# Cross attention and routed experts on one core: x of five batches transposed by the DMA crossbar, and a rebuilt opening

## The chip, the cores and the metric

The kernel runs on 1 core of a Trainium2 chip. Five engines work side by side, each with its own queue of instructions in order: TensorE (PE, with its weight loads PEld), VectorE (DVE), ScalarE (ACT), GpSimd (POOL) and SyncE (SP, which only issues DMAs). The core has 16 DMA engines. DMAs are issued from SP's queue, from ACT's, or from GpSimd's (software-generated, which can cast). The metric is the device time of the program in microseconds (us), as the median of the runs.

## The reference

Two stages. The first is an attention between x and a small state in both directions, for 8 batches and 8 heads, with S = 512, 32 state rows and D = 64:

```
scores  = scale * x @ state^T        ;  xread = softmax(scores)  @ state      (512 rows per batch)
scores2 = scale * state @ x^T        ;  sread = softmax(scores2) @ x          (32 rows per batch)
x2 = [xread, sread] as rows: 8 * 544 = 4352 rows of 512
```

The second is a mixture of 8 experts over these rows, in which every expert computes every row, and the weights P are balanced by 8 rounds of row and column normalisation (Sinkhorn):

```
P = exp(x2 @ w_gate - max), 8 rounds:  P /= row sums;  P /= column sums;  P *= N / E
out = sum over e of  P[:, e] * (relu(x2 @ w1[e]) @ w2[e])        w1: 512 x 1024, w2: 1024 x 512
```

The output has 4352 x 512 values in float32.

## The kernel before

**Heads.** Four of a batch's eight heads are worked at once, so there are 16 objects `Heads(k)`, two per batch: k = 2b + q. "Head k" below means such a group of four. Its steps are:

- `transpose` (L168): eight TensorE transposes of 128x128 (`xT_ps`), and one VectorE copy to `xT`
- `scores` (L178): two matmuls `sc_ps` of state (`stT`, 64 columns each) with `xT`; ScalarE takes exp with row sums to `E2`
- `rows` (L189): reciprocal `rrec` and normalised `En` on VectorE
- `columns` (L196): matmul `den_ps` with a matrix of ones, then Ln and Exp on ScalarE to `rcp`
- `flip` (L203): four transposes of `En` to `ET_ps`, copied to `ET` by VectorE
- `weights` (L210): `AT` = E2 times rcp on VectorE
- `read_x` (L213): eight matmuls `su_ps` of `x_nat` with `ET`, copied to `xs`

`beat(k)` (L482) strings head k's steps together with the transposes and scores of head k+1.

**Expert 0 beside attention.** xread is never formed: the product of state and W1 (`G`, from matmuls `g_ps`) is computed first, and layer 1 then multiplies `AT` with `G` (`hps`, then relu on ScalarE to `hT`). `state_times_w1(bp, w1h)` (L285) computes `G` for a pair of batches, in eight steps of one 128x512 product, whose two halves of 64 partitions go to the two batches in one copy each. For the first pair the copies of five steps are on ScalarE and of three on VectorE, for later pairs all are on VectorE. `layer1` (L335) has eight steps per batch, `layer2` (L357) has for each of four row tiles two steps of four matmuls (`yps`), and a copy to `acc`.

**Order.** All engine queues are written out by hand (`manual_schedule`): program order is queue order. After the hand-written start (the "opening", heads 0 and 1), `prologue` is the list of attention steps, cut into parts of two heads, and `units[c]` is the list of expert steps (layer 1 of batch c, layer 2 of batch c-1, and the `G` of a later pair). `weave` mixes a unit with its part of the prologue. I call such a mixture a unit below. Later experts (1 to 7) follow with a layer 2 of fewer products (`layer2_winograd`); the change doesn't touch them.

**Loads.** State and x come on SP's queue (`load_state` L83, `load_x` L92), in tiles `x_st` with three buffers, of which the two state tiles (`st_nat`) are two turns. `cast_x` (L100) makes fp16 `x_nat` (three buffers), on VectorE for batches 0 and 1 and on GpSimd after that. Weights come with a cast on GpSimd's queue (`load_w1`, `load_w2`). The start is gated so that they come one after another: a one-element copy on GpSimd holds W1 until the state is there, x of batch 1 until W1's first half is there, and W2 until W1's second half is there. `ahead(b)` (L553) stands at the first head of batch b-1, loads and casts x of batch b, and at b = 5 also starts the weights of expert 1. `prepare_state(g)` (L145) casts and transposes the state of four batches. `warm(n)` (L497) issues matmuls without a purpose but activity.

**The end of the attention stage** is near 122 us of the profile; after it SP carries the `G<-raw` copies of the later experts.

Of the kernel before, what the change touches and what calls it, by code (L numbers as in the profile page):

```python
# [10 lines left out]
FP32 = mybir.dt.float32  # L11
FP16 = mybir.dt.float16
# [6 lines left out]
def kernel(  # L19
# [9 lines left out]
    nc = tc.nc  # L29

    B, H, S, D = x.shape
    Ns = state.shape[2]
    Dm, E = moe_w_gate.shape
    F = moe_w1.shape[2]
    SB = S + Ns
    N = B * SB
    NKC = Dm // 128
    NFB = F // 128
    NTB = N // 128
    NSC = S // 128  # L40
    NQ = H // 4
    SR = B * S

    inv_sqrt_d = 1.0 / float(D) ** 0.5
# [3 lines left out]
    psM = ctx.enter_context(tc.tile_pool(name="psM", bufs=4, space=bass.MemoryType.PSUM))  # L48
# [6 lines left out]
    gp = ctx.enter_context(tc.tile_pool(name="gp", bufs=4))  # L55
# [7 lines left out]
    AT = persist.tile([128, NQ, SR], FP16, name="AT")  # L63
# [11 lines left out]
    actx = ExitStack()  # L75
    axs = actx.enter_context(tc.tile_pool(name="attn_xs", bufs=3))
    axp = actx.enter_context(tc.tile_pool(name="attn_x", bufs=3))
    asb = actx.enter_context(tc.tile_pool(name="attn_sb", bufs=2))
    ast = actx.enter_context(tc.tile_pool(name="attn_st", bufs=1))
    stT = ast.tile([128, B // 2, NKC, 2, 64], FP16, name="stT")  # L80
    st_nat = [axs.tile([128, H, D], FP32, name=f"st_nat{g}", tag="x_st") for g in range(2)]

    def load_state(g):  # L83
        for k in range(4):
            nc.sync.dma_start(out=st_nat[g][ds(32 * k, 32)],
                              in_=state[4 * g + k].rearrange("h n d -> n h d"))


    x_st = {}
    x_nats = {}  # L90

    def load_x(b, after=None):  # L92
        xv = x[b].rearrange("h (p s) d -> p h s d", s=NSC)
        for q in range(NQ):
            t = x_st[b, q] = axs.tile([128, 4, NSC, D], FP32, name="x_st", tag="x_st")
            if after is not None and q == 0:
                nc.gpsimd.tensor_copy(out=t[:1, 0, 0, :1], in_=after)
            nc.sync.dma_start(out=t, in_=xv[:, ds(4 * q, 4)])

    def cast_x(b, q):  # L100
        if q == 0:
            x_nats[b] = axp.tile([128, NKC, NSC, 2, D], FP16, name="x_nat", tag="x_nat")
        for par in range(2):
            (nc.vector if b < 2 else nc.gpsimd).tensor_copy(
                out=x_nats[b][:, 2 * q + par].rearrange("p s i d -> p i s d"),
                in_=x_st[b, q][:, ds(2 * par, 2)])

    def load_w1(e, after=None):
        w1h = mw.tile([128, NKC, F], FP16, name="w1h", tag="w1h")
# [51 lines left out]
    class Heads:  # L161
# [4 lines left out]
            self.odd = self.b % 2  # L166

        def transpose(self):  # L168
            xn = x_nats[self.b]
            xT_ps = psA.tile([128, 2, S], FP16, name="xT_ps", tag="a")  # L170
            for par in range(2):
                for sc in range(NSC):
                    nc.tensor.transpose(xT_ps[:, par, ds(128 * sc, 128)],  # L173
                                        xn[:, 2 * self.q + par, sc, :, :], identh)
            self.xT = asb.tile([128, 2, S], FP16, name="xT", tag="xT")
            nc.vector.tensor_copy(out=self.xT, in_=xT_ps)  # L176

        def scores(self):  # L178
# [34 lines left out]
        def read_x(self):  # L213
            xn = x_nats[self.b]
            su_ps = psA.tile([128, 2, 64], FP32, name="su_ps", tag="a")
            for par in range(2):
                for sc in range(NSC):
                    nc.tensor.matmul(su_ps[:, par, :], xn[:, 2 * self.q + par, sc, :, :],  # L218
                                     self.ET[:, sc, ds(64 * (par ^ self.odd), 64)],
                                     start=(sc == 0), stop=(sc == NSC - 1))  # L220
            for i in range(2):
                nc.vector.tensor_copy(
                    out=xs[ds(64 * i, 64), ds(2 * self.q, 2), ds(self.b * Ns, Ns)],
                    in_=su_ps[ds(64 * i, 64), :, ds(32 * i, 32)])
# [28 lines left out]
    def state_times_w1_four(g, w1h, split=False):  # L253
# [5 lines left out]
        def step(kc, fhs):  # L259
# [15 lines left out]
            if 1 in fhs:  # L275
                for b in range(4):
# [5 lines left out]
        return G, [partial(step, kc, fhs) for kc in range(NKC)  # L282
                   for fhs in ([(0,), (1,)] if split else [(0, 1)])]

    def state_times_w1(bp, w1h):  # L285

        G = []

        def step(kc, fh):
            if not G:  # L290
                G.extend(gp.tile([128, NQ, F], FP16, name="G", tag="G") for _ in range(2))
            g_ps = psM.tile([128, 512], FP32, name="g_ps", tag="m")
            nc.tensor.matmul(g_ps, stT[:, bp, kc, :, :], w1h[:, kc, ds(512 * fh, 512)])  # L293
            on_dve = bp > 0 or (kc, fh) in ((0, 0), (2, 0), (1, 1))
            evac = nc.vector.tensor_copy if on_dve else nc.scalar.copy
            for half in range(2):
                evac(out=G[half ^ (kc % 2)][ds(64 * half, 64), kc // 2, ds(512 * fh, 512)],  # L297
                     in_=g_ps[ds(64 * half, 64), :])

        return G, [partial(step, kc, fh) for fh in range(F // 512) for kc in range(NKC)]  # L300

# [33 lines left out]
    def layer1(c, w1h, G):  # L335

        tn = S if c < B else B * Ns
        h = []

        def step(fb):  # L340
            if not h:
                h.append((mh if c < B else mhs).tile([128, NFB, tn], FP16, name="hT", tag="hT"))
            hps = psM.tile([128, 512], FP32, name="hps", tag="m")
            if c < B:
                for q in range(NQ):
                    nc.tensor.matmul(hps[:, :tn], G[c % len(G)][:, q, ds(fb * 128, 128)],  # L346
                                     AT[:, q, ds(c * S, S)],
                                     start=(q == 0), stop=(q == NQ - 1))
            else:
                for kc in range(NKC):  # L350
                    nc.tensor.matmul(hps[:, :tn], w1h[:, kc, ds(fb * 128, 128)], xs[:, kc, :],  # L351
                                     start=(kc == 0), stop=(kc == NKC - 1))
            nc.scalar.activation(out=h[0][:, fb, :], in_=hps[:, :tn], func=AF.Relu)  # L353

        return h, [partial(step, fb) for fb in range(NFB)]
# [104 lines left out]
    def weave(a, b):  # L460

        steps, k = [], 0
        for i, f in enumerate(a):
            steps.append(f)
            while k < len(b) and k * len(a) < (i + 1) * len(b):
                steps.append(b[k])
                k += 1
        return steps + b[k:]

    def run(steps):  # L470
        for f in steps:
            f()
# [7 lines left out]
    heads = [Heads(k) for k in range(B * NQ)]  # L480
# [9 lines left out]

    warm_sb = ast.tile([128, S], FP16, name="warm_sb")
    nc.vector.memset(warm_sb, 0.0)
    warm_ps = psM.tile([128, S], FP32, name="warm_ps", tag="m")

    def warm(n):  # L497
        for _ in range(n):
            nc.tensor.matmul(warm_ps, warm_sb[:, :128], warm_sb)  # L499
# [3 lines left out]
    warm(11)  # L503
    identh = consts.tile([128, 128], FP16, name="identh")
    make_identity(nc, identh)
    headones = consts.tile([128, 128], FP16, name="headones")
    nc.vector.memset(headones, 0.0)
    for h in range(4):
        nc.vector.memset(headones[ds(32 * h, 32), ds(32 * h, 32)], 1.0)
    nc.gpsimd.memset(stT, 0.0)  # L510
    w1h = load_w1(0, st_nat[0][:1, 0, :1])

    prepare_state(0)
# [3 lines left out]
    w2h = load_w2(0, w1h[:1, 0, F // 2:F // 2 + 1])  # L517
# [1 line left out]
    nc.gpsimd.memset(ones128, 1.0)  # L519
    wgh = consts.tile([128, NKC, E], FP16, name="wgh")  # L520
    nc.gpsimd.dma_start(out=wgh, in_=moe_w_gate.rearrange("(kc p) e -> p kc e", p=128))
    Gs, first = state_times_w1(0, w1h)
    warm(6)
    heads[0].transpose()
    cast_x(0, 1)
    warm(3)
    heads[0].scores()
    warm(1)
    heads[1].transpose()
    heads[0].rows()  # L530
    warm(1)
    heads[0].columns()
    warm(3)
    heads[0].flip()
    heads[1].scores()
    heads[0].weights()
    heads[0].read_x()
    heads[1].rows()
    warm(1)
    heads[1].columns()  # L540
    warm(1)
    heads[1].flip()
    heads[1].weights()
    run(first[:3])
    heads[1].read_x()
    for f in first[3:6]:
        f()
        warm(1)
    cast_x(1, 0)
    run(first[6:])  # L550
    cast_x(1, 1)

    def ahead(b):  # L553
        if b < B:
            load_x(b)
            cast_x(b, 0)
            cast_x(b, 1)
        if b == B - 3:
            w_nxt.extend(load_w(1))

# [14 lines left out]
    rest = [lambda: (sinkhorn_columns(), sinkhorn_rows()) for _ in range(7)] + [sinkhorn_columns]  # L575

    units = []
    last = []
    for c in range(B + 1):
        if c % 2 == 0:  # L580
            G = Gs
            gs = []
            if c + 2 < B:
                Gs, gs = state_times_w1(c // 2 + 1, w1h)
        h, l1 = layer1(c, w1h, G)
        units.append(weave(weave(last, l1), gs[4 * (c % 2):][:4]))
        last = layer2(0, c, h, w2h)
    units.append(last)
    cut[-1] = len(prologue)
# [14 lines left out]
    Gs, gs = state_times_w1_four(0, W[1][0], True)  # L604
# [16 lines left out]
    h, l1, g = begin(*order[0])  # L621
# [3 lines left out]
    s, p = layer2_winograd(*order[0], h, W[1][1], wt[1])  # L625
# [3 lines left out]
    for i, (e, c) in enumerate(order):  # L629
# [9 lines left out]
        h, l1, g = begin(e1, c1)  # L639
# [13 lines left out]
        s, p = s1, p1  # L653
# [28 lines left out]
```

The softmax here doesn't subtract the row's maximum and nothing guards it: scores larger than these inputs give would overflow.

## Time and profile before

| What | us |
|---|---|
| median of 10 runs | 779.68 (779.29 to 783.54) |
| the profiled execution's own time | 781.63 |
| its span, first to last instruction | 779.8 |
| TensorE busy | 762.4 |
| VectorE busy | 620.2 |
| ScalarE busy | 492.2 |
| GpSimd busy | 42.3 |

In the page of the profile, engines are rows, times are us from the start of the span, and "busy" is the time in which an instruction of the engine is recorded. TensorE's matmuls overlap each other, and their ends are modelled: eight 128x128 transposes show 219 ns each and take 0.45 us together. In the chain of work that ended last, each piece is put down with its start, its length, its engine, the tile that it writes and its line. In the answer by stretches, each line has the stretch, its length, the busy us and the number of instructions for PE, PEld, DVE, ACT and POOL, then the granted TensorE clock (1.00 is full), the busy share of the DMA engines and GB/s.

### The profile page before, as it was taken

How to read it: one execution, taken by the hardware profiler on the slowest of the kernel's cores; microseconds unless marked ns; L12 is line 12 of the kernel's file. 1: busy time of each engine (PE TensorE's matmuls, PEld its weight loads, DVE VectorE, ACT ScalarE, POOL GpSimd, SP SyncE). 2: the span in 40 equal slices, each digit the busy share in tenths (PEclk: the TensorE clock that was granted, in tenths of full speed). 3: DMA queues.
4: the chain of work that ended last, by engine and by line, in shares of the span. 5: the costliest groups of instructions: out<-in, count | busy, mean ns of one | idle time of the engine just before them, and what ended most of it. 6: DMA issues, size and time to landing. Idle time of an engine off the chain costs nothing.

```text
span 779.8 us, 15072 instructions
## 1 busy us (share of the span) xinstructions
PE 762.4 (98%) x5630; PEld 505.6 (65%) x5630; DVE 620.2 (80%) x1357; ACT 492.2 (63%) x946; POOL 42.3 (5%) x68
## 2 busy tenths in 40 slices
PE   8899999999999999999999999999999999999997
PEld 3444444566677666766677676766667667767774
DVE  5767666988888888888888888888888888887885
ACT  5666666598886666476665666466665666565542
POOL 3231100000001000000001000010001000000000
PEclk9999999999999999999999999999999999999999
DMA  9765001571127222182225422192224521123434
GB/s 209 196 171 100 1 2 31 111 143 49 49 54 124 70 53 55 35 155 55 55 56 94 97 55 55 29 162 56 52 54 80 114 51 50 38 54 133 126 109 149
DMA packets 54617, 64.96 MB, mean 83 GB/s; under 512 B 11280, under 2 KB 35856, under 8 KB 54544
## 3 DMA queue, kind: packets, MB, share of 16 engines
q1 hardware_dynamic: 37120, 47.22, 21.4%
q0 software_dynamic: 17424, 16.79, 14.3%
q8 instruction: 44, 0.72, 0.4%
q14 instruction: 29, 0.24, 0.1%
HBM read 42.48 MB, written 8.91 MB: 66 GB/s over the span
## 4 chain that ended last, share of the span: by engine, by line
PE 95%; DVE 3%; ACT 1%; issue 0%
PE hps L346 28%; PE ra L415 27%; PE rx L415 20%; PE yps L367 8%; PE g_ps L271 4%; PE hps L351 4%; DVE G L297 1%; PE warm_ps L499 1%; PE g_ps L293 1%; PE xT_ps L173 1%; PE sc_ps L182 1%; ACT G L297 1%; PE ET_ps L206 1%; DVE xT L176 1%; ACT raw L274 1%; PE su_ps L218 0%
## 5 line engine op out<-in xcount | busy, mean ns | idle before, releaser
L353 ACT ACTIVATE hT<-hps 128x512 f16<-128x512 f32 (+1 forms) x576 | 318.5, 579 | 216.5 <-PE hps L346 141.0
L346 PE MATMUL hps<-AT,G 128*128 128x512 f16 x1024 | 283.5, 379 | 4.0 <-ACT raw L274 3.2
L421 DVE SCALAR_TENSOR_TENSOR acc<-ra,Pmat,acc 128x256 f32<-128x256 f32 x468 | 219.5, 478 | 71.9 <-PE ra L415 71.2
L415 PEld LDWEIGHTS <-sm 128*128 128x128 f16 x1872 | 182.6, 98 | 65.4 <-DVE sm L401 2.1
L421 DVE SCALAR_TENSOR_TENSOR acc<-rx,Pmat,acc 128x256 f32<-128x256 f32 x351 | 168.4, 480 | 32.2 <-PE rx L415 19.9
L415 PEld LDWEIGHTS <-hT 128*128 128x128 f16 x1404 | 133.7, 98 | 57.9 <-issue 18.7
L415 PE MATMUL ra<-wt,sm 128*128 128x256 f16 x936 | 140.5, 273 | 0.2
L274 ACT CAST raw<-g_ps 128x512 f16<-128x512 f32 x224 | 115.4, 598 | 31.1 <-PE g_ps L271 29.0
L346 PEld LDWEIGHTS <-G 128*128 128x128 f16 x1024 | 97.5, 98 | 54.3 <-issue 11.0
L401 DVE TENSOR_TENSOR sm<-hT 128x1024 f16<-128x1024 f16 (+1 forms) x124 | 80.7, 651 | 0.6 <-ACT hT L353 0.6
L367 PE MATMUL yps<-w2h,hT 128*128 128x512 f16 x304 | 76.9, 379 | 0.0
L415 PE MATMUL ra<-w2h,hT 128*128 128x256 f16 x468 | 70.6, 273 | 0.0
L415 PE MATMUL rx<-w2h,hT 128*128 128x256 f16 x468 | 70.2, 273 | 0.0
L415 PE MATMUL rx<-wt,sm 128*128 128x256 f16 x468 | 70.2, 273 | 0.0
L415 PE MATMUL rx<-w2h,sm 128*128 128x256 f16 x468 | 70.2, 273 | 0.0
L415 PE MATMUL ra<-wt,hT 128*128 128x256 f16 x468 | 61.2, 273 | 0.0
L367 PEld LDWEIGHTS <-hT 128*128 128x128 f16 x304 | 28.8, 98 | 32.7 <-issue 1.8
L297 DVE CAST G<-g_ps 64x512 f16<-64x512 f32 x54 | 37.1, 686 | 13.2 <-PE g_ps L293 12.7
L401 DVE TENSOR_TENSOR sm<-hT,sm 128x1024 f16<-128x1024 f16 (+1 forms) x62 | 40.4, 651 | 0.2
L401 DVE TENSOR_TENSOR sm<-sm,hT 128x1024 f16<-128x1024 f16 (+1 forms) x62 | 40.3, 650 | 0.0
L114 POOL DMA_DIRECT2D w1h<-in_moe_w_dram x16 | 12.0, 755 | 472.9 <-PE hps L351 472.6
L271 PE MATMUL g_ps<-w1h,stG 64*128 64x512 f16 x224 | 35.0, 382 | 0.2 <-ACT hT L353 0.2
(76 smaller groups left out, 380.4 us busy)
## 6 DMA issues: line engine op xcount, KB each, us to landing
G<-raw SPq DMA_DIRECT2D x448, 64.0 KB, 2.0
x_st<-in_x_dram SPq DMA_DIRECT2D x16, 512.0 KB, 4.4
w1h<-in_moe_w_dram POOLq DMA_DIRECT2D x16, 512.0 KB, 7.5
w2h<-in_moe_w_dram POOLq DMA_DIRECT2D x16, 512.0 KB, 8.8
out_dram<-acc SPq DMA_DIRECT2D x32, 256.0 KB, 2.6
st_nat<-in_state_dram SPq DMA_DIRECT2D x8, 64.0 KB, 3.7
out_dram<-acc SPq DMA_DIRECT2D x8, 64.0 KB, 1.7
wgh<-in_moe_w_gate_dram POOLq DMA_DIRECT2D x1, 8.0 KB, 8.5
```

The source lines that it names most:

```text
L114: nc.gpsimd.dma_start(out=w1h[:, :, fs], in_=w1r[e, :, :, fs])
L173: nc.tensor.transpose(xT_ps[:, par, ds(128 * sc, 128)], xn[:, 2 * self.q + par, sc, :, :], identh)
L271: nc.tensor.matmul(t, stG[ds(64 * i, 64), g, kc, :], w1h[ds(64 * i, 64), kc, ds(512 * fh, 512)])
L274: nc.scalar.copy(out=raw[kc][:, i, ds(512 * fh, 512)], in_=t)
L297: evac(out=G[half ^ (kc % 2)][ds(64 * half, 64), kc // 2, ds(512 * fh, 512)], in_=g_ps[ds(64 * half, 64), :])
L346: nc.tensor.matmul(hps[:, :tn], G[c % len(G)][:, q, ds(fb * 128, 128)], AT[:, q, ds(c * S, S)], start=(q == 0), stop=(q == NQ - 1))
L351: nc.tensor.matmul(hps[:, :tn], w1h[:, kc, ds(fb * 128, 128)], xs[:, kc, :], start=(kc == 0), stop=(kc == NKC - 1))
L353: nc.scalar.activation(out=h[0][:, fb, :], in_=hps[:, :tn], func=AF.Relu)
L367: nc.tensor.matmul(yps[tk], h[0][:, fb, ds(tk * 128, 128)], w2h[:, fb, :], start=(fb == 0), stop=(fb == NFB - 1))
L401: op(sm[k], *[sm[v] if isinstance(v, int) else a(*v) for v in (x, y)])
L415: nc.tensor.matmul(r[nm, i], lhs[:, k, ds(128 * i, 128)], rhs[:, k, :], start=(first and k == 0), stop=(k == FH - 1), skip_group_check=True)
L421: nc.vector.scalar_tensor_tensor(out=dst, in0=r[nm, i], scalar=Pmat[:, t + i, e:e + 1], in1=dst, op0=ALU.mult, op1=ALU.add)
```

## The change

- **Crossbar.** For batches 3 to 7 (`XB = 3`) x is no longer transposed on TensorE. After the casts, `transpose_x(b)` stores `x_nat` to a DRAM tile `xh` (512 x 4 x 128, fp16, three buffers) from GpSimd's queue, and a transposing DMA on SP's queue loads it to `xT`. `xT` is now one tile per batch (128 x 4 x 512) with two buffers. The layout of `x_nat` has its two middle dimensions exchanged. For batches 0 to 2 the transposes stay on TensorE.
- **Loads.** Two of the four state loads of the first group and the first half of x(0) are issued from ScalarE's queue. The second state tile has a buffer of its own, and x(b+1) is loaded after the casts of batch b.
- **Opening.** Batches 0 and 1 get a `G` each from `state_times_w1_one`: four steps of two 64-column products and one 128x512 copy, on ScalarE for q = 0 and on VectorE for q = 1. Four layer-1 steps of batch 0 are placed among heads 0 and 1, and half of its layer 2 moves one unit ahead. For the next pair (bp = 1) one of each two half copies goes to ScalarE. Nine `warm` matmuls are gone. The zeroing of `stT` moves from GpSimd to VectorE, and the filler reads a part of `AT` that is not yet used.

```diff
+    XB = 3
...
+    axt = actx.enter_context(tc.tile_pool(name="attn_xt", bufs=2))
+    dram = actx.enter_context(tc.tile_pool(name="dram", bufs=3, space=bass.MemoryType.DRAM))
...
-    st_nat = [axs.tile([128, H, D], FP32, name=f"st_nat{g}", tag="x_st") for g in range(2)]
+    st_nat = [axs.tile([128, H, D], FP32, name="st_nat0", tag="x_st"),
+              ast.tile([128, H, D], FP32, name="st_nat1")]
...
-            nc.sync.dma_start(out=st_nat[g][ds(32 * k, 32)],
-                              in_=state[4 * g + k].rearrange("h n d -> n h d"))
+            (nc.scalar if g == 0 and k > 1 else nc.sync).dma_start(
+                out=st_nat[g][ds(32 * k, 32)],
+                in_=state[4 * g + k].rearrange("h n d -> n h d"))
...
-            nc.sync.dma_start(out=t, in_=xv[:, ds(4 * q, 4)])
+            (nc.scalar if b + q == 0 else nc.sync).dma_start(out=t, in_=xv[:, ds(4 * q, 4)])
...
-            x_nats[b] = axp.tile([128, NKC, NSC, 2, D], FP16, name="x_nat", tag="x_nat")
+            x_nats[b] = axp.tile([128, NSC, NKC, 2, D], FP16, name="x_nat", tag="x_nat")
...
+    def transpose_x(b):
+        xh = dram.tile([S, NKC, 128], FP16, name="xh", tag="xh")
+        nc.gpsimd.dma_start(out=xh.rearrange("(s p) k c -> p s k c", p=128),
+                            in_=x_nats[b].rearrange("p s k i d -> p s k (i d)"))
+        xTs[b] = axt.tile([128, NKC, S], FP16, name="xT", tag="xT")
+        nc.sync.dma_start_transpose(xTs[b], xh)
...
         def transpose(self):
+            if self.q == 0 and self.b < XB:
+                xTs[self.b] = axt.tile([128, NKC, S], FP16, name="xT", tag="xT")
+            self.xT = xTs[self.b][:, ds(2 * self.q, 2)]
+            if self.b >= XB:
+                return
...
-            self.xT = asb.tile([128, 2, S], FP16, name="xT", tag="xT")
...
+    def state_times_w1_one(b, w1h):
+        G = []
+        def step(q, fh):
+            if not G:
+                G.append(gp.tile([128, NQ, F], FP16, name="G", tag="G"))
+            g_ps = psM.tile([128, 512], FP32, name="g_ps", tag="m")
+            for par in range(2):
+                half = par ^ (b % 2)
+                nc.tensor.matmul(g_ps[ds(64 * half, 64), :], stT[:, b // 2, 2 * q + par, half, :],
+                                 w1h[:, 2 * q + par, ds(512 * fh, 512)])
+            (nc.vector.tensor_copy if q else nc.scalar.copy)(
+                out=G[0][:, q, ds(512 * fh, 512)], in_=g_ps)
+        return G, [partial(step, q, fh) for fh in range(F // 512) for q in range(NQ)]
...
-            on_dve = bp > 0 or (kc, fh) in ((0, 0), (2, 0), (1, 1))
-            evac = nc.vector.tensor_copy if on_dve else nc.scalar.copy
             for half in range(2):
-                evac(out=G[half ^ (kc % 2)][ds(64 * half, 64), kc // 2, ds(512 * fh, 512)],
-                     in_=g_ps[ds(64 * half, 64), :])
+                (nc.scalar.copy if bp == 1 and half else nc.vector.tensor_copy)(
+                    out=G[half ^ (kc % 2)][ds(64 * half, 64), kc // 2, ds(512 * fh, 512)],
+                    in_=g_ps[ds(64 * half, 64), :])
...
-    warm_sb = ast.tile([128, S], FP16, name="warm_sb")
+    warm_sb = AT[:, NQ - 1, ds(SR - S, S)]
...
+    nc.vector.memset(stT, 0.0)
...
-    nc.gpsimd.memset(stT, 0.0)
...
-    Gs, first = state_times_w1(0, w1h)
+    G0, g0 = state_times_w1_one(0, w1h)
+    G1, g1 = state_times_w1_one(1, w1h)
     warm(6)
     heads[0].transpose()
     cast_x(0, 1)
     warm(3)
     heads[0].scores()
-    warm(1)
     heads[1].transpose()
     heads[0].rows()
     warm(1)
     heads[0].columns()
-    warm(3)
+    heads[1].scores()
+    run(g0[:2])
     heads[0].flip()
-    heads[1].scores()
     heads[0].weights()
+    heads[1].columns()
     heads[0].read_x()
     heads[1].rows()
-    warm(1)
-    heads[1].columns()
-    warm(1)
+    heads[1].weights()
+    run(g0[2:3])
     heads[1].flip()
-    heads[1].weights()
-    run(first[:3])
+    h, l1 = layer1(0, w1h, G0)
+    run(l1[:2] + g0[3:])
     heads[1].read_x()
-    for f in first[3:6]:
-        f()
-        warm(1)
     cast_x(1, 0)
-    run(first[6:])
+    run(weave(l1[2:4], g1[:2]))
     cast_x(1, 1)
+    load_x(2)
...
     def ahead(b):
         if b < B:
-            load_x(b)
             cast_x(b, 0)
             cast_x(b, 1)
+            if b + 1 < B:
+                load_x(b + 1)
+            if b >= XB:
+                transpose_x(b)
...
-    last = []
-    for c in range(B + 1):
-        if c % 2 == 0:
-            G = Gs
-            gs = []
-            if c + 2 < B:
-                Gs, gs = state_times_w1(c // 2 + 1, w1h)
-        h, l1 = layer1(c, w1h, G)
-        units.append(weave(weave(last, l1), gs[4 * (c % 2):][:4]))
+    Gp[1], gs = state_times_w1(1, w1h)
+    last = layer2(0, 0, h, w2h)
+    units.append(weave(l1[4:], g1[2:]) + weave(last[:4], gs[:2]))
+    last, gs = last[4:], gs[2:]
+    for c in range(1, B + 1):
+        if c in (2, 4):
+            Gp[c // 2 + 1], gs = state_times_w1(c // 2 + 1, w1h)
+        gc = gs if c == 1 else gs[4 * (c % 2):][:4] if c < B - 2 else []
+        h, l1 = layer1(c, w1h, G1 if c == 1 else Gp.get(c // 2))
+        units.append(weave(weave(last, l1), gc))
         last = layer2(0, c, h, w2h)
```

More of the change, by code (lines that the diff above doesn't have):

```diff
@@ L77 @@
     axp = actx.enter_context(tc.tile_pool(name="attn_x", bufs=3))
+    axt = actx.enter_context(tc.tile_pool(name="attn_xt", bufs=2))
     asb = actx.enter_context(tc.tile_pool(name="attn_sb", bufs=2))
+    dram = actx.enter_context(tc.tile_pool(name="dram", bufs=3, space=bass.MemoryType.DRAM))
     ast = actx.enter_context(tc.tile_pool(name="attn_st", bufs=1))
     stT = ast.tile([128, B // 2, NKC, 2, 64], FP16, name="stT")
-    st_nat = [axs.tile([128, H, D], FP32, name=f"st_nat{g}", tag="x_st") for g in range(2)]
+    st_nat = [axs.tile([128, H, D], FP32, name="st_nat0", tag="x_st"),
+              ast.tile([128, H, D], FP32, name="st_nat1")]
     def load_state(g):
         for k in range(4):
-            nc.sync.dma_start(out=st_nat[g][ds(32 * k, 32)],
-                              in_=state[4 * g + k].rearrange("h n d -> n h d"))
+            (nc.scalar if g == 0 and k > 1 else nc.sync).dma_start(
+                out=st_nat[g][ds(32 * k, 32)],
+                in_=state[4 * g + k].rearrange("h n d -> n h d"))
     x_st = {}
+    xTs = {}
     x_nats = {}
@@ L97, in load_x @@
                 nc.gpsimd.tensor_copy(out=t[:1, 0, 0, :1], in_=after)
-            nc.sync.dma_start(out=t, in_=xv[:, ds(4 * q, 4)])
+            (nc.scalar if b + q == 0 else nc.sync).dma_start(out=t, in_=xv[:, ds(4 * q, 4)])
     def cast_x(b, q):
         if q == 0:
-            x_nats[b] = axp.tile([128, NKC, NSC, 2, D], FP16, name="x_nat", tag="x_nat")
+            x_nats[b] = axp.tile([128, NSC, NKC, 2, D], FP16, name="x_nat", tag="x_nat")
         for par in range(2):
             (nc.vector if b < 2 else nc.gpsimd).tensor_copy(
-                out=x_nats[b][:, 2 * q + par].rearrange("p s i d -> p i s d"),
+                out=x_nats[b][:, :, 2 * q + par].rearrange("p s i d -> p i s d"),
                 in_=x_st[b, q][:, ds(2 * par, 2)])
+    def transpose_x(b):
[4 more added lines that the diff above has]
+        nc.sync.dma_start_transpose(xTs[b], xh)
     def load_w1(e, after=None):
@@ L173, in transpose @@
                     nc.tensor.transpose(xT_ps[:, par, ds(128 * sc, 128)],
-                                        xn[:, 2 * self.q + par, sc, :, :], identh)
-            self.xT = asb.tile([128, 2, S], FP16, name="xT", tag="xT")
+                                        xn[:, sc, 2 * self.q + par, :, :], identh)
             nc.vector.tensor_copy(out=self.xT, in_=xT_ps)
@@ L217, in read_x @@
                 for sc in range(NSC):
-                    nc.tensor.matmul(su_ps[:, par, :], xn[:, 2 * self.q + par, sc, :, :],
+                    nc.tensor.matmul(su_ps[:, par, :], xn[:, sc, 2 * self.q + par, :, :],
                                      self.ET[:, sc, ds(64 * (par ^ self.odd), 64)],
@@ L577 @@
     units = []
-    last = []
-    for c in range(B + 1):
-        if c % 2 == 0:
-            G = Gs
-            gs = []
-            if c + 2 < B:
-                Gs, gs = state_times_w1(c // 2 + 1, w1h)
-        h, l1 = layer1(c, w1h, G)
-        units.append(weave(weave(last, l1), gs[4 * (c % 2):][:4]))
+    G, Gp = None, {}
+    Gp[1], gs = state_times_w1(1, w1h)
[8 more added lines that the diff above has]
+        units.append(weave(weave(last, l1), gc))
         last = layer2(0, c, h, w2h)
```

## The prediction

> **What bounds the kernel now.** I read the totals first, then the chain of work that ended last, then the busy time by stretch around the attention stage, which is where the change acts.
>
> ```profile
> PE 762.4 (98%) x5630; PEld 505.6 (65%) x5630; DVE 620.2 (80%) x1357; ACT 492.2 (63%) x946; POOL 42.3 (5%) x68
> PE 95%; DVE 3%; ACT 1%; issue 0%
> x_st<-in_x_dram SPq DMA_DIRECT2D x16, 512.0 KB, 4.4
> ```
>
> TensorE is on the chain for 95% of the span. The rest (5%, some 35 us) is not spread out. Stretches of the attention stage, columns: stretch, length, busy us (instructions) of each engine, granted clock, DMA share, GB/s:
>
> ```profile
> 10.00:20.00 10.00, 7.14 (x54) 3.27 (x53) 8.01 (x20) 7.90 (x16) 2.90 (x6) 1.00 1.09 236
> ...
> 20.40:24.10 3.70, 3.70 (x17) 1.64 (x17) 1.86 (x5) 1.73 (x3) 0.00 (x0) 0.56 1.33 247
> ...
> 30.00:35.00 5.00, 3.60 (x29) 1.57 (x26) 4.38 (x9) 3.35 (x7) 2.35 (x4) 1.00 0.60 200
> ...
> 33.90:48.10 14.20, 14.20 (x103) 7.28 (x102) 11.97 (x30) 10.66 (x26) 2.65 (x5) 1.00 0.52 155
> 48.10:62.90 14.80, 13.51 (x126) 6.98 (x124) 9.01 (x23) 8.90 (x20) 5.18 (x8) 1.00 0.96 205
> ```
>
> Up to 33 us TensorE has holes and filler (warm_ps), and a stretch at about half clock; from 33.9 on it has almost none. So before 33 us time is won by making work available earlier, after it only by taking work off TensorE, as long as no other engine is pushed over its time. The chain shows both:
>
> ```profile
> 15.15 0.58 ACT G L297
> ...
> 19.77 0.59 ACT G L297
> 20.36 0.04 issue
> 20.40 0.61 PE hps L346 x2
> 21.01 0.43 PE warm_ps L499
> 21.44 0.85 PE xT_ps L173 x8
> 22.29 1.28 PE warm_ps L499 x3
> 23.57 0.57 PE sc_ps L182 x2
> ...
> 42.79 0.45 PE xT_ps L173 x8
> 43.23 0.43 PE hps L346 x2
> 43.67 0.86 PE yps L367 x4
> ```
>
> From 15 to 20.4 us layer 1 of batch 0 waits for ScalarE to copy G out of PSUM, ten copies at 0.58. In the dense part eight transposes hold TensorE for 0.45 us (0.85 at the low clock).
>
> **Transposes removed.** Heads 6 to 15 (batches 3 to 7) lose 80 transposes on TensorE, 10 x 0.45 = 4.5 us, and 10 copies xT on VectorE (128x1024, 0.692 us each), 6.9 us. Head 6 falls in a stretch that ScalarE will bound (below), so I count nine: **4.0 us**. VectorE's 6.9 us lie beside TensorE work except in one place: at 55.98 the xT copy stands ahead of En, and TensorE idles 0.71 before ET. That goes: **0.7 us**. If TensorE were not the bound in these stretches, the 4.0 would be worth nothing.
>
> **What takes their place.** Per batch: one 512 KB store xh from GpSimd's queue after the casts, and one transposing load on SP's queue. On GpSimd the next casts stand behind each store's issue; the profile's SWDGE issues of that size take 0.75 us, and its casts have idle time of 8 us and more before them. On SP's queue the transposing load waits for xh and for the scores of batch b-2 (two xT buffers). Queued behind it: x of batch b+2, whose casts come a batch later, and at the end the G<-raw copies, which start near 122 us. The load for batch 3 is the tightest. Both halves of x(3) are issued near 21 us, as the separate st_nat1 frees a buffer. They land behind x(2) and W2 at some 29 us (before: casts at 31.1 and 33.1 waited for them). Casts 1.2, issue 0.75 and some 5 us of store (W1's SWDGE loads of 512 KB take 7.5 with the DMA full, x loads 4.4) put xh at 36. Scores of head 6 should come at 44.4. So the transfer has 8.4 us; batch 4 has 12 and later ones more, with one due about every 14 us.
>
> The trace has no transposing load. The nearest row is a plain load of the same 512 KB: 4.4 us. [...]
>
> **The opening.** State and x(0) are issued from SP and ACT together. The first scores (9.42) wait for xT, the end of a row x(0), cast, transposes, copy. Total bytes are the same and W1 shares the DMA from 4 us, so I give it 0, between -0.7 and +0.8 (ACT's issues may stand behind its 1.28 us table load). The stT memset (1.80 on GpSimd) moves to VectorE, by its rows (0.11 at 64, 0.27 at 256 elements) 0.9 us, finished before VectorE first has data at 5.1: 0.
>
> Then the order. Batch 0's G is four 128x512 copies, shared by ScalarE and VectorE (about 0.59 and 0.69), instead of a share of 16 half-height ones; layer 1's first steps need two of them. By hand with the profile's durations: scores of head 1 at 11.35 instead of 12.17; the first two G products 11.75 to 12.5 (W1's first half lands at 11.5); head 0's ET, read, head 1's ET until 15.4; layer 1 steps 0 and 1 from 15.5 instead of 20.4; head 2's transposes at 19.3, its scores at 21.0 instead of 23.57. Cost: 16 products of 64 columns, in pairs at 0.34 as scores are, 2.7 us against 8 x 0.216 = 1.7, paid in idle time. Then layer 1's rest and half of layer 2 of batch 0 run among heads 2 and 3, ending (read of head 3) at 30.4 instead of 34.1, with four more layer-2 groups done (4 x 0.86 = 3.4 us) and two G products fewer (0.4).
>
> **ScalarE takes half of that back.** Half of pair 1's G copies move to it (8 x 0.58). Between the starts of E for head 4 and for head 6 and through the latter it has 7 relus x 0.597, 5 G x 0.581, 3 acc x 0.588, 4 Ln/Exp x 0.59, 3 E with their read at 0.793, and stT and stG, 1.5: sum 15.1 us. TensorE's own work there is about 11. From 30.15 that gives 45.2; before, E of head 6 ended at 47.98, with the same work done. With 0.5 us of gaps the opening is worth **2.3 us**, not the 6.6 that TensorE alone would say. After that the unit of two heads is TensorE's again (ACT 10.3 of 15 us).
>
> W2 is now needed at 25.2 (first half) and 26.9 (second). It was issued at 14.56 and 15.3, landing in 6.5 and 8.3 us; half of x(2), 0.5 MB at the 235 GB/s of this stretch, can come ahead of it, 2.2 us: at worst 23.3 and 25.8. Hidden, by 1 us.
>
> Nine warm matmuls go. The clock: before, it fell to 0.56 at 20.4 after 3.4 us with TensorE busy 1.6. [...]
>
> **Sum.** 4.0 + 0.7 + 2.3 = 7.0 us off the profiled span of 779.8 (its execution took 781.63). The median of the runs is 779.68; the same difference gives **772.6**.
>
> **Rivals.**
> - **Half of it is lost, 776.5.** Either ScalarE's gaps, a late W2 or a clock drop eat the opening (then 4.7 remain, less a little), or a crossbar load of 9 to 11 us delays head 6 by 1 to 3. For it: the 1 us margin of W2 and the 15.1 us of ScalarE. Against: VectorE is relieved at the same time.
> - **The crossbar is slow, slower than before.** Heads 6 and 8 wait for xT. [...] Against: the row of 4.4.
> - **ScalarE doesn't bind, 769.** G's copies slip between relus, and all of the 6.6 minus some waits arrives.
> - **No effect.** Transposes and copies were covered anyway and the opening gains nothing: against it stands a dense TensorE on the chain.
>
> **How the numbers follow.** Chances: main case 0.53 (own range 770.3 to 774.8), half lost 0.22, slow crossbar 0.13 (half of it below 785), ScalarE free 0.09, no effect 0.03. The range of 8 in 10 takes in the halved case and leaves out most of the slow crossbar and the far end of the free case: 768.5 to 780. Within 0.2% (1.6 us, about what this kernel's measurement can tell from no change): no effect, 0.03; faster 0.53 + 0.22 + 0.09 = 0.84; slower 0.13.
>
> **What would show it.** Right: no wait of sc_ps (L182 before) for a DMA; SP's transposing loads landing in under 8 us; scores of head 2 near 21 and E of head 6 near 45 us; units of two heads after 50 us shorter by about 0.9 each; TensorE's clock 1.0 between 20 and 25. Wrong: scores or E waiting for xT from DMA, ScalarE idle between 30 and 45 us, yps waiting for w2h, or GpSimd's casts late behind a store.

## The result, and the profile after

The changed kernel takes 773.97 us (median, 773.12 to 775.57) against 779.69 before: a ratio of 0.9923, 95% interval 0.9913 to 0.9932, or 5.7 us. The forecast was 772.6.

The totals of the changed kernel, and its chain by engine:

```profile
PE 755.7 (98%) x5549; PEld 499.7 (65%) x5549; DVE 608.7 (79%) x1338; ACT 492.9 (64%) x948; POOL 44.6 (6%) x72
...
PE 95%; DVE 2%; ACT 2%; issue 0%; ACTq 0%
```

TensorE has lost 6.7 us of busy time, VectorE 11.5, and TensorE still sets the end. The same kernel by stretches (length, busy us of PE, PEld, DVE, ACT, POOL, clock, DMA share, GB/s):

```profile
10.00:20.00 10.00, 8.27 (x69) 3.75 (x67) 7.65 (x22) 7.68 (x16) 2.78 (x6) 1.00 1.10 259
...
20.40:24.10 3.70, 3.24 (x25) 1.47 (x25) 1.97 (x6) 3.03 (x7) 0.89 (x2) 1.00 1.21 230
...
30.00:35.00 5.00, 4.93 (x40) 2.46 (x38) 3.19 (x9) 4.18 (x9) 1.83 (x3) 1.00 0.86 285
...
33.90:48.10 14.20, 11.79 (x100) 5.38 (x98) 8.71 (x26) 13.03 (x30) 7.14 (x12) 1.00 0.63 180
```

The holes up to 35 us are mostly filled, and the clock stays at 1.00 where it had been 0.56. In exchange TensorE now idles 2.4 us between 33.9 and 48.1, where it had idled none, and there ScalarE is busy 13.0 of 14.2. The chain of the changed kernel shows the new opening and the new wait:

```profile
15.36 0.86 PE hps L380 x4
...
20.60 0.41 PE sc_ps L200 x2
...
39.67 0.59 ACT stG L173
...
40.28 0.58 ACT G L330
```

Layer 1 starts at 15.4 instead of 20.4, scores of head 2 at 20.6 instead of 23.5. The start of the scores, which stands on TensorE's own queue, is the best ruler for the attention stage (both profiles start head 0's scores at 9.4):

| Start of scores, us | head 2 | head 6 | head 7 | head 8 | head 15 |
|---|---|---|---|---|---|
| before | 23.50 | 46.41 | 58.80 | 63.68 | 116.31 |
| changed | 20.60 | 42.74 | 53.84 | 58.12 | 107.71 |
| ahead | 2.9 | 3.7 | 5.0 | 5.6 | 8.6 |

From head 8 to 15 the lead grows by 3.0 us in seven heads, 0.43 each. But 8.6 is more than the 5.7 of the medians. The two profiled executions are 8.2 apart (781.63 and 773.39), since the profiled run of before was not a typical one: it took 781.63 against a median of 779.7. The third group of experiments comes back to that. SyncE's queue in the changed kernel (start, us of the issuing, what):

```profile
35.34 1.95 SPq L120 DMA_TRANSPOSE xT<-xh  x1
...
45.79 1.98 SPq L120 DMA_TRANSPOSE xT<-xh  x1
...
54.28 12.12 SPq L120 DMA_TRANSPOSE xT<-xh  x1
```

No wait of TensorE for a crossbar load is in this profile. The third load (batch 5), though, takes 12 us to be issued.

### The profile page after: what moved, and what is told of

Same layout as the page of the kernel before. It is cut to its first block, busy times and chain, and to the rows that moved or that the text cites. A ratio compares the mean times of both kernels' runs of the same rounds, so it can differ in the third digit from the quotient of the medians.

```text
span 771.5 us, 14909 instructions
## 1 busy us (share of the span) xinstructions
PE 755.7 (98%) x5549; PEld 499.7 (65%) x5549; DVE 608.7 (79%) x1338; ACT 492.9 (64%) x948; POOL 44.6 (6%) x72
## 4 chain that ended last, share of the span: by engine, by line
PE 95%; DVE 2%; ACT 2%; issue 0%; ACTq 0%
PE hps L380 28%; PE ra L449 27%; PE rx L449 20%; PE yps L401 8%; PE g_ps L289 4%; PE hps L385 4%; PE warm_ps L533 1%; DVE G L330 1%; PE sc_ps L200 1%; PE g_ps L328 1%; ACT raw L292 1%; PE ET_ps L224 1%; DVE xT L194 0%; PE su_ps L236 0%; PE den_ps L216 0%
## 5 line engine op out<-in xcount | busy, mean ns | idle before, releaser
L330 DVE CAST G<-g_ps 64x512 f16<-64x512 f32 x40 | 27.4, 686 | 19.0 <-PE g_ps L328 18.7
L128 POOL DMA_DIRECT2D w1h<-in_moe_w_dram x16 | 12.1, 760 | 468.0 <-PE hps L385 467.4
```

The lines of the kernel that those rows point to most:

```text
L128: nc.gpsimd.dma_start(out=w1h[:, :, fs], in_=w1r[e, :, :, fs])
L330: (nc.scalar.copy if bp == 1 and half else nc.vector.tensor_copy)(out=G[half ^ (kc % 2)][ds(64 * half, 64), kc // 2, ds(512 * fh, 512)], i ...
```

## The experiments

### One part at a time

No crossbar, the opening alone:

```diff
-    XB = 3
+    XB = 8
```

> The changed kernel with all transposes left on TensorE (no crossbar), so the new opening alone. Main theory (ScalarE takes back most of what the opening wins): 2.3 us below the kernel before, 777.4, with TensorE waiting for ScalarE between 35 and 45 us. Rival (ScalarE doesn't bind, the opening is worth 5 to 6): 774. Rival (the opening is worth nothing against the median, since the profiled run of before had a stretch at half clock that most runs have not): 779.5.

Measured 778.22 us, ratio to before 0.9974 (0.9963 to 0.9985): the opening alone is worth 1.5 us, less than expected but more than nothing. Its profiled execution (778.38) is 3.25 faster than that of before (781.63), and its scores of head 15 start at 112.05 instead of 116.31. TensorE waits for ScalarE at 41 us, once and for 1.2, as expected. The crossbar on top of the opening is worth 4.25 (778.22 to 773.97), where the prediction had 4.7.

The crossbar for three batches instead of five:

```diff
-    XB = 3
+    XB = 5
```

> The changed kernel with the crossbar for batches 5 to 7 only; batches 3 and 4 are transposed on TensorE again. Main theory (TensorE sets the pace, 0.45 us per group of eight transposes, head 6 hidden under ScalarE, 0.7 at head 7): slower than the changed kernel by 3 x 0.45 + 0.7 = 2.0 us, 776.0; faster than with no crossbar by 6 x 0.45 = 2.7. Rival (the copies on VectorE are what counts, 0.69 per head): slower by 2.8 and faster by 4.1. Rival (the later transfers contend with the weights of expert 1): no difference to the changed kernel, 774.

Measured 776.93 (0.9957, 0.9944 to 0.9969). By medians that is 3.0 slower than the changed kernel and 1.3 faster than no crossbar. The sum, 4.3, is near the 4.7 of the main theory and far from the 6.9 of VectorE's copies. The split is not as expected: 3.0 and 1.3, where the theory had 2.0 and 2.7. The traces, read at the scores of head 15 (107.71 changed, 109.50 here, 112.05 without crossbar), say 1.8 and 2.55, close to the theory. They leave out what comes after the attention stage, where the time from these scores to the end differs between single profiles by up to 1.3 us; but each is one execution, so the split of the medians stays unexplained. What leaves TensorE is some 0.43 us per head, and VectorE's copies are covered.

One term of the prediction was a single wait of 0.71 us at head 7, which was to go with the xT copy. It is there in the kernel before and without crossbar, and with the crossbar most of it stays. In this order, before, opening alone, changed:

```profile
57.18 0.40 PE L206 MATMUL ET_ps<-identh,En 128*128 128x128 f16 x4 [0.71 <-DVE En L193]
...
52.91 0.40 PE L224 MATMUL ET_ps<-identh,En 128*128 128x128 f16 x4 [0.71 <-DVE En L211]
...
52.22 0.40 PE L224 MATMUL ET_ps<-identh,En 128*128 128x128 f16 x4 [0.56 <-DVE En L211]
```

The crossbar path alone in the kernel before:

```diff
+    XB = 3
...
+            if b >= XB:
+                transpose_x(b)
```

> The kernel before with only the crossbar path for batches 3 to 7 (old opening, old split of the G copies; x of the next batch is loaded ahead of the store). Main theory: 4.5 (ten heads, as ScalarE doesn't bind here) + 0.7 = 5.2 us below the kernel before, 774.5. Rival (parts overlap: the opening and the crossbar win the same wait at head 6): the two parts alone sum to more than the 5.7 of both. Rival (xT of batch 3 comes late without the separate state buffer): under 4.

Measured 777.15 (0.9963, 0.995 to 0.9977): 2.6 us, a miss. With the opening's 1.5 the parts sum to 4.1, less than the 5.7 of both, so neither does the overlap rival hold. The gap of 1.6 is hardly more than what the three intervals, of about 1 us each way, leave room for. Its profile, with the same clock dip as that of before (0.56 from 20.4 to 24.1), has the scores of head 15 at 111.70 against 116.31: 4.6 us, near the expected 5.2; the two executions (777.43 and 781.63) are 4.2 apart. In that run the gain arrived, in the median it did not.

One attempt at this gap, the weights of expert 1 later (below, with the same edit in the changed kernel):

> The kernel before with the crossbar path alone, and expert 1's weights loaded at b = 7. Theory (with the old opening too, the transposing load of batch 5 waits out the weights, and this took away the part of the expected 5.2 us that was not measured, 2.6 of them): 775.0 to 775.6, 1.6 to 2.2 faster than the crossbar path with early weights. Rival (the missing part is work that was covered anyway): 777.

Measured 777.58 (0.9976, 0.996 to 0.9992, two of twelve runs at 782 and above): no gain, the theory fell, although the load of batch 5 (58.03) was issued in 1.9 us; with early weights it took 10.6 (57.98) and 15.9 to land. Its profile shows something else, the load of batch 3:

```profile
40.35 2.16 SPq L118 DMA_TRANSPOSE xT<-xh  x1
```

It needs 4.5 us, so xT of batch 3 lands at 44.9; scores of head 6 come at 45.8, in a run with the clock dip (mean clock 0.997). Without the dip they would be ready some 2 us earlier, and xT would be late. Some of the runs fit this: those with a mean clock of 0.997 took 777.5 to 777.7 and those at 1.0 took 777.2, so that the dip, which costs some 2 us in the kernel before, would cost little here. The others scatter (776.8 to 782.7), and no trace without the dip was kept, so the late xT is argued, not shown. In the changed kernel the same load starts 5 us earlier, since the second state tile has a buffer of its own and x of batch 3 is loaded sooner. That would cover part or all of the 1.6 us that the parts lack; a run with only that buffer added was not made, so the gap stays open.

### How much room the crossbar has

```diff
-        nc.sync.dma_start_transpose(xTs[b], xh)
+        for _ in range(2):
+            nc.sync.dma_start_transpose(xTs[b], xh)
```

> The changed kernel with every transposing load issued twice into the same tile, so that xT comes one transfer later. In the trace of the changed kernel the load for batch 3 is issued at 35.3 and needs 4 to 5.5 us, while scores of head 6 come at 42.7: a margin of 2 to 3 us. Main theory (transfers are hidden by that margin at batch 3 and by more at the others): batch 3 late by about 2 us, total 1 to 3 us slower than the changed kernel, 776. Rival (the loads were on the path already): 5 x 4.5, over 20 us slower. Rival (the margin is larger than a transfer): no difference, 774.

Measured 781.38 (1.0014, 1.0001 to 1.0026): 7.4 us slower than the changed kernel, far more than expected, and just slower than before. The wait of TensorE (total, times, longest), and the stretches around it:

```profile
PE sc_ps L201 <- DMA xT<-xh: 5.8, 2, 4.2
```

```profile
42.00:46.00 4.00, 0.28 (x2) 0.11 (x1) 0.00 (x0) 2.23 (x4) 0.00 (x0) 1.00 1.14 281
46.00:50.00 4.00, 3.53 (x17) 1.53 (x17) 1.71 (x4) 1.87 (x4) 1.97 (x4) 0.58 1.16 330
```

The second load is issued at 39.83, 4.5 us after the first, and 4.5 is also the median of these loads from issue to landing, so I take it that it waits for the first to land. xT of batch 3 lands at 46.4 instead of 39.8. Scores of head 6 move from 42.7 to 46.5: the margin was 2.9 us, as the expectation said, but the second transfer took 6.6. The expectation also left out that after an idle stretch of 4.2 us TensorE's granted clock is 0.66 from 46 to 48, 0.50 from 48 to 50 and 0.99 from 50 to 52: scores of head 7 are 5.0 us late (58.80 for 53.84), 1.2 more than those of head 6. A second wait of 1.6 us stands at head 10 (batch 5).

The same with `range(3)`:

> Every transposing load issued three times into the same tile, a transfer of some 13 to 16 us. By the prediction's own sum it breaks even with the kernel before at 13.8 us: 776 to 784 expected, with waits of scores for xT at batch 3 (6 to 8 us) and a smaller one at batch 4. Rival (transfers are hidden everywhere): 774.

Measured 792.38 (1.0155, 1.0138 to 1.0171), 18.4 us slower than the changed kernel, outside what was expected:

```profile
PE sc_ps L201 <- DMA xT<-xh: 16.0, 3, 7.7
```

```profile
50.00:54.00 4.00, 3.72 (x17) 1.59 (x17) 1.38 (x4) 1.87 (x4) 1.36 (x3) 0.50 1.07 301
72.00:78.00 6.00, 2.97 (x15) 1.29 (x15) 0.45 (x2) 1.29 (x3) 0.88 (x2) 0.50 1.20 279
```

Three waits of 16.0 us in all, and two stretches at half clock. The expectation had a small wait at batch 4; it was the longest, 7.7, as the three loads of batch 4 (issued from 49.22 to 70.33) ran beside the weights of expert 1 and landed at 75.0. With two loads, a transfer of 11.1 us at batch 3 (35.35 to the scores that waited for it, 46.47), with the second wait at batch 5, was already past the break-even. The prediction's room of 8.4 us at batch 3 and 12 at batch 4, against its 7.0 us in all, puts that near 13.8 (late by 5.4 and 1.8), by estimate.

The third load of the changed kernel, alone in its window (kind of issue, count, us from issue to landing), is the one that was slow to issue:

```profile
xT<-xh SPq DMA_TRANSPOSE x1, 17.3
```

It runs beside the weights of expert 1 (the last of them lands at 69.9) and itself lands at 71.6; scores of head 10 start at 71.80. Loading these weights after the last store takes the company away:

```diff
-        if b == B - 3:
+        if b == B - 1:
             w_nxt.extend(load_w(1))
```

> The changed kernel with the weights of expert 1 loaded after the last crossbar store (at b = 7) instead of at b = 5. In the trace of the changed kernel the transposing load of batch 5 runs beside these weights, needs 17.3 us and lands at 71.6, while scores of head 10 are at 71.9. Theory (in some runs it lands late, and this is the spread of 773.1 to 775.6): all transposing loads land in under 7 us, the runs lie within 0.6 us of each other, median 773.2, 0.5 to 0.8 faster than the changed kernel. Rival (the margin of 0.2 us always holds, the spread has another cause): median and spread unchanged, 774.0.

Measured 773.41 (0.9917, 0.9902 to 0.9932), the runs from 773.21 to 774.54. The same load and the next one now:

```profile
xT<-xh SPq DMA_TRANSPOSE x2, 4.3
```

The last load, of batch 7, now has the weights beside it. SyncE's queue shows it with the one before:

```profile
65.36 22.87 SPq L120 DMA_TRANSPOSE xT<-xh  x2
```

It starts before 80 and is issued until 88.23, so the issuing alone takes over 8 us, where those of batches 3 to 5 take 1.9 to 2.0. The slow load goes where the weights go, so they made the difference between 4.3 and 17.3 us. The two other things that the theory expected did not come: not all loads were under 7 us, and the runs still lie 1.3 us apart. That the median is better by 0.56 is inside the intervals, so that the changed kernel ever waited for this load is not shown.

### ScalarE, VectorE and the clock

The half copies of G for the second pair back on VectorE:

```diff
-                (nc.scalar.copy if bp == 1 and half else nc.vector.tensor_copy)(
+                nc.vector.tensor_copy(
```

> The changed kernel with the half copies of G for the second pair back on VectorE (8 x 0.58 off ScalarE, 8 x 0.69 onto VectorE). Main theory (ScalarE binds between 30 and 45 us: it is busy 9.5 of 10 us there, and TensorE idles 1.8): faster than the changed kernel by 1 to 2 us, 772.5. Rival (VectorE then puts both copies ahead of xT and En, as in the kernel before): the same or up to 1.5 us slower.

Measured 777.26 (0.9967, 0.9955 to 0.9979), 3.3 us slower than the changed kernel: my theory fell, and the loss is over twice what the rival gave. TensorE's waits between 30 and 60 us, here:

```profile
PE ET_ps L224 <- DVE En L211: 1.5, 3, 0.8
PE lg_ps L250 <- DVE Gg L266: 1.4, 1, 1.4
PE t_ps L164 <- DVE st_h L161: 1.3, 1, 1.3
PE g_ps L328 <- DVE G L330: 0.7, 1, 0.7
```

and in the changed kernel:

```profile
PE g_ps L328 <- ACT G L330: 1.5, 1, 1.5
PE lg_ps L250 <- DVE Gg L266: 0.6, 1, 0.6
PE ET_ps L224 <- DVE En L211: 0.6, 1, 0.6
PE t_ps L164 <- DVE st_h L161: 0.3, 1, 0.3
```

ScalarE's wait of 1.5 goes and four on VectorE grow, from 1.5 to 4.9 us: the pairs of G copies (1.38 us each) are now in VectorE's queue, and at 41.1 one of them stands ahead of En. That is 1.9 of the 3.3 us; where the rest is lost was not traced.

Half of them, with the stG copy moved too:

```diff
-                (nc.scalar.copy if bp == 1 and half else nc.vector.tensor_copy)(
+                (nc.scalar.copy if bp == 1 and half and fh else nc.vector.tensor_copy)(
...
-        nc.scalar.copy(out=stG[:, g], in_=t_ps)
+        (nc.vector.tensor_copy if g else nc.scalar.copy)(out=stG[:, g], in_=t_ps)
```

> The changed kernel with only the second column half's G copies of the second pair on ScalarE (4 instead of 8), and the stG copy of the second state group on VectorE: 4 x 0.58 + 0.59 = 2.9 us off ScalarE, 4 x 0.69 + 0.4 to 0.7 onto VectorE. Main theory (ScalarE binds from 30 to 45 us): faster than the changed kernel by 1 to 2 us, 772.5, and no worse than with all copies on VectorE. Rival (the pace there is set by the chain of TensorE, VectorE and ScalarE around prepare_state, not by ScalarE's load): within 0.5 us of the changed kernel.

Measured 776.87 (0.9953, 0.9935 to 0.9971): 2.9 slower, neither theory. Its profile has a cause that neither named. TensorE is busy only 1.9 of the 4 us from 40 to 44, with a wait of 2.1 for ScalarE's half of G, and then the clock falls:

```profile
44.00:46.00 2.00, 2.00 (x7) 0.48 (x5) 0.35 (x2) 1.92 (x4) 0.00 (x0) 0.50 0.65 264
```

So in this execution a part of the loss is the clock, and how much was not separated. And the stG copy alone, with late weights:

> The changed kernel with late weights as above, and the stG copy of the second state group on VectorE instead of ScalarE (0.59 us off the row of ScalarE copies at 38 to 41 us for which TensorE waits 1.5 us at a g_ps buffer). Theory (ScalarE's order around prepare_state is a bound there): 0.4 to 0.6 faster than with late weights alone, 772.7. Rival (VectorE, with st_h, stT and G before En, becomes the later one, as when G's copies were moved to it): same or up to 1 us slower.

Measured 775.29 (0.9934, 0.992 to 0.9948, the two edits shown above together): 1.9 slower than with late weights alone. The two of its six runs with a mean clock of 1.0 took 773.8 and 774.2, the others, at 0.997 to 0.999, 775.1 to 775.9, so here too the clock can have a share. The timeline of this kernel says why 0.59 us off ScalarE don't help (start, us, what, idle before and what ended it):

```profile
38.66 0.93 ACT L170 COPY stT<-t_ps 64x128 f16<-64x128 f16 x4 [0.18 <-PE hps L380]
39.62 0.42 DVE L173 COPY stG<-t_ps 128x512 f16<-128x512 f16 x1 [1.05 <-ACT stT L170]
39.96 0.67 DVE L330 CAST G<-g_ps 64x512 f16<-64x512 f32 x1
...
40.67 0.58 ACT L330 CAST G<-g_ps 64x512 f16<-64x512 f32 x1 [1.08 <-DVE G L330]
```

stG waits for ScalarE's copies of the same t_ps, holds VectorE's half of G behind it, and ScalarE's half of G starts only after VectorE's half. TensorE then waits 2.0 us for the g_ps buffer instead of 1.5. At this place the two engines form one chain through shared tiles, and the load of either isn't its length.

More filler in the kernel before:

```diff
     for f in first[3:6]:
         f()
-        warm(1)
+        warm(3)
...
-    run(first[6:])
+    for f in first[6:]:
+        f()
+        warm(3)
```

> The kernel before with 3 instead of 1 filler matmuls between the first G products, and 3 more after each of the last two, all in time where TensorE waits for ScalarE. Theory (the half-clock stretch at 20 to 24 us of the profiled run comes from the busy share before it and is in some runs only): runs near 781.5 go away, the median falls by at most 0.3, clock 1.0 at 20 to 24. Rival (the stretch is in most runs): median falls by 1 to 1.9 us. Rival (the clock has another cause): nothing changes.

Measured 780.2 (0.9998, 0.9988 to 1.0007): the median doesn't fall, and the whole range is 779.61 to 780.39. The first line here is the stretch of the kernel before ahead of its clock of 0.56, with TensorE busy 1.60 of 3.40 us. Then come the two stretches of this kernel, in which the clock stays at 1.00:

```profile
17.00:20.40 3.40, 1.60 (x7) 0.48 (x5) 3.27 (x7) 3.29 (x7) 0.00 (x0) 1.00 1.23 204
...
17.00:20.40 3.40, 3.40 (x17) 1.54 (x16) 3.27 (x9) 3.10 (x6) 0.00 (x0) 1.00 1.26 218
20.40:24.10 3.70, 3.56 (x29) 2.00 (x28) 2.46 (x6) 2.74 (x6) 0.00 (x0) 1.00 1.34 267
```

The kernel before, in the runs beside these experiments, has a group at 779.2 to 780.2 with a mean clock of 0.999 or 1.0, and a group from 781.4 up (17 of 62) with 0.995 to 0.998. With filler that second group is gone; at its share of 17 in 62, eleven runs without one would come by chance in 3 cases of 100. So the half-clock stretch is in about one run of four and costs some 2.2 us there, and TensorE's low activity before it (busy 1.60 of 3.40 us, against 3.40 with filler) is by these runs very likely what sets it off; the profiled run of before was one of those.

## Why the prediction was right, step by step

The main case came true, 5.7 us for 7.0, but the closeness owes something to luck: in the opening two errors, of about 2 and 1 us, have opposite signs.

- **What bounds the kernel: right.** TensorE on the chain before and after, holes before 33 us, most of them filled after. Per-head gain 0.43 us for 0.45.
- **Transposes removed, 4.0 + 0.7: 4.25 measured.** The 4.0 fits the 0.43 per head. The 0.7 was wrong: the wait at head 7 shrank from 0.71 to 0.56 only. Without the xT copy (0.69) En ends earlier by as much, but without its eight transposes TensorE also comes to this wait about 0.5 earlier. I had counted both in full; head 7 gains 0.6 (11.70 us between the scores of heads 6 and 7 with the opening alone, 11.10 in the changed kernel), and 4.0 + 0.15 is near the 4.25.
- **Crossbar hidden: right, by less than I wrote.** Taken 4.4 us from the plain load of 512 KB, so 0; measured 4.5, 5.5 and 4.2 in the changed kernel where no weights ran beside it (batches 3, 6 and 7), and 6.7 for batch 4, whose load had the first of them beside it. For batch 3 I gave the transfer 8.4 us of room; it had 7.4 (35.3 to 42.7). For batch 5 I saw ample room and did not put the weights of expert 1 beside it: 17.3 us, with 0.2 to spare. My own sign of being right, all transposing loads under 8 us, failed there.
- **Opening, 2.3: 1.5 measured, the step that was mis-sized.** The times were met: scores of head 2 predicted at 21.0, found at 20.6; read of head 3 at 30.4 and 30.2; end of E of head 6 at 45.2 (45.7 with the gaps) and 45.4. The fault is in what they were compared with, twice. The 47.98 of before stands in a profile that took 781.63, and I subtracted the difference from a median of 779.68: some 2 us of it are a clock stretch that the median has not. I had named the half-clock stretch, but not asked whether the median had it. And at that mark I wrote "with the same work done", which is wrong: by then TensorE has run 36 instead of 32 `yps`, 32 instead of 30 `hps` and 8 more `su_ps`. With the opening alone the lead is 2.5 us at this mark and 4.3 at the scores of head 7, where layers 1 and 2 have the same count again, and it stays at 4.3 until head 15. After the attention stage 1.0 of it is lost again in that execution, for a reason that stays open. So the opening won 3.25 us against the profiled run and 1.5 against the median. Of the 1.3 us between forecast and result 0.8 is here, and 0.45 in the crossbar's term.
- **ScalarE takes half back: a wait is there, its size was wrong.** The stretch is 13.0 of 14.2 us full of ScalarE, and TensorE waits for it. But TensorE idles 2.4 us there, where the prediction let ScalarE take 4.3 (6.6 less 2.3); 6.6 less 2.4 is near the lead of 4.3 in the traces. And three versions that took work off ScalarE were slower by 1.9 to 3.3 us (in two of them the clock may have a share): the chain runs through VectorE as well.
- **W2 and the clock: right.** TensorE waits for no weights at the first yps (24.5), and the clock stays at 1.00.
- **The slow-crossbar rival: right in kind, its turning point wrong.** Not 13.8 us but under 11.1, as the room was smaller (7.4) and as I left out the clock after a wait (0.58 over the 4 us after one of 4.2) and that the load of batch 5 meets the weights. The part of its chance beyond 785 was an estimate of mine for a slower load that no run shows: the single loads of the changed kernel landed in 4.2 to 17.3 us and held up no scores.

## What to carry to other kernels

Before subtracting from a profile, ask where its own execution lies among the runs: here a clock stretch of one run in four was in the picture and not in the median. When two schedules are compared at a mark, count what lies behind it in both. Work taken off the bound engine paid at its rate here (0.43 us a head, for transposes of 0.45), as long as the new path kept its room when other transfers ran beside it (4.2 us for a load alone, 17.3 beside weights); measure that room by doubling the transfer. And an engine that is nearly full is not yet the cause: where two engines pass copies through the same tiles, moving one from the fuller to the emptier lengthened the chain here (TensorE's wait went from 1.5 to 2.0 us).

## What was not expected of the hardware

- A transposing load of 512 KB landed in 4.2 to 5.5 us without weight loads beside it (changed kernel, batches 3, 6 and 7; with late weights the median of batches 5 and 6 is 4.3), and in 17.3 beside two pairs of casting weight loads (changed kernel, batch 5); its issue then held SyncE's queue for 12.1 us instead of 2.0.
- TensorE's clock fell to 0.56 in the profile of before (20.4 to 24.1) after a stretch in which it was busy 1.6 of 3.4 us, with no hole over 0.82 us; by the run times this is so in about one run of four, and in none of eleven with filler in the holes. In the changed kernel, busy 2.7 of 4.5 us from 36.9 to 41.4, it stayed at 1.00. A hole of 4.2 us, as in the doubled load, brought 0.58 over the next 4 us.
- Where ScalarE and VectorE copy two halves of one PSUM tile, ScalarE's half never began before VectorE's had ended (eight pairs in the changed kernel, 0.03 us or more after; and at 40.67 above). Where ScalarE had idled before its half, three times of the eight, the profile names VectorE's copy as what released it, so I take it that the program's order asks for this; whether the two could run at the same time was not tried.
